# Splitting the tap sums in two and moving four early steps in a fused convolution and maxout kernel

## The chip, the cores and the metric

The kernel runs on one core of one Trainium2 chip. The metric is the time of one execution on the device, in microseconds (us), as the median of several runs; lower is better. A separate execution was profiled: its profile gives the start and the length of nearly every instruction on the core's engines, and of the DMA packets.

The engines are written as in the profile: PE multiplies matrices (PEld is its loading of the stationary operand), DVE works on vectors, ACT applies functions and copies, POOL and SP here mostly issue DMAs.

## The reference

The input x has 8 sequences of 4160 rows with 192 values. Each row also has 8 heads x 7 logits. A softmax over the 7 logits gives weights for the row itself and the six before it, head by head; then the 33280 rows go through a layer that takes the maximum of two products:

```python
w = np.exp(weight_gen - max); w = w / (sum over the 7 taps + 1e-09)
out = np.einsum('bshk,bskhg->bshg', w, x_unf)      # 7 taps, 8 heads x 24 values
...
h1 = x @ w1                                        # 192 -> 1024
h2 = x @ w2
g = np.maximum(h1, h2)
return (g @ w_out).astype(np.float32)              # 1024 -> 192
```

## The kernel before

**Tiling.** Each of the 128 partitions holds 260 consecutive rows ("columns" of 128 rows each). Batches of 16 columns are the unit of the softmax; units of 4 columns (the first 32 columns, units 0 to 7) or 8 columns (the rest) are the unit of the convolution. One column's worth of the layer is a *tile*: 260 tiles, worked off in groups, of two tiles up to tile 15 (groups 0 to 7) and of three tiles after that.

**The layer.** The maximum is written as h1 + relu(h2 - h1). `hid_tile(t)` (line 352) makes the tile's 1024 hidden values on PE from the convolved columns `yt` and from `wd` = w2 - w1, `relu(rd, t, n)` (line 362) takes them through ACT into `rd`, and the result of a column is 16 products of `rd` with `wo`, the bf16 copy of w_out (line 392), plus 3 products of `yt` with `w10` = w1 @ w_out (line 405). Halves of the PE array work side by side on 64 rows each, so `wd` exists with its halves of rows in place (blocks 0 to 2) and swapped (blocks 3 to 5). `halves_swapped(frm, bank)` makes a swapped block: one product into a PSUM bank, then a copy on ACT (lines 677 and 679).

**The convolution.** Per batch: `exp_sum` (ACT, line 162), `red` (DVE, 180), `ln` (ACT, 186), `shift` (DVE, 191), `weights` (ACT, 202: the normalised weights in bf16, twice each), `mul` (DVE, 218: all 7 taps of a unit into `m_t`). From unit 8 on DVE adds up the taps (`adds`, 244 to 253) and a DMA transposes the sum (262). For units 0 to 7 `sum_transpose(u)` (line 285) does both on PE: for each of six blocks k, seven taps and two halves it is a 64-column product of `m_t` with the identity (line 296), 84 products in all (48 for unit 5, whose taps DVE adds up in part), and ACT then copies the result to `yt` (line 304).

**What sets the order.** Every engine works off its instructions in the order in which the program states them; waits come from the data, from PSUM banks that must be read out before they are filled again, and from explicit ties: `behind(first, load)` makes a DMA's issue wait for `first`. The first 16 tiles and their softmax are written out by hand, from line 698 on. PSUM in that stretch is two pools of two buffers each, `h` (hidden tiles; also `pw`) and `o` (`yps` of a tap sum, `op_ps` of results, `other`, `tp`). In `hidden(g, ...)` (line 543) the order on PE is: the group's first hidden tile, the first half of the previous results (`out_first`), the second hidden tile, the second half (`out_second`), the copy of the results by ACT (`evac`, line 478), and then what the caller passes as `between`. A callback `ahead` runs between the second relu and `out_second`.

The places that the change touches, before it:

- POOL issues the DMA of `wo` (line 706) right behind a load of x, with no wait; `wo` is first read by `out_hidden_only(OUTS[3])` at line 781.
- Lines 722 to 744: on ACT the order is relu of tile 0, relu of tile 1, `ln(0)`, `exp_sum(1)`, the copy of swapped block 4 (`halves_swapped(1, other)`), `weights(0, 8)`, the copy of unit 1's sum, `ln(1)`, relu of tile 2. `hid_tile(2)` is the first that reads block 4.
- Lines 778 to 786: `sum_transpose(2)` as a whole, then `out_hidden_only`, `hid_tile(6)`, `out_hidden_rest`, relu of tile 6, `hid_tile(7)`.
- Lines 889 to 896: the tap sums of units 4, 6 and 7 stand in `between` of groups 4, 6 and 7. In group 4, `weights(1, 12)` is the `ahead` step, and `exp_sum(2)` and `red(2)` stand in `between`, behind the copy of the results.

Of the kernel before, what the change touches and what calls it, by code (L numbers as in the profile page):

```python
# [9 lines left out]
FP32 = mybir.dt.float32  # L10
# [13 lines left out]
def kernel(  # L24
# [133 lines left out]
    def exp_sum(b, i=0, of=1):  # L158
        if i == 0:
            e_ts[b] = pe_.tile([P, BATCHES[b][1] * WGC], FP32, name="e_t", tag="e")  # L160
        w = BATCHES[b][1] * WGC // of
        return nc.scalar.activation(out=e_ts[b][:, i * w:(i + 1) * w], in_=wg_ts[b][:, i * w:(i + 1) * w], func=AF.Exp)  # L162
# [15 lines left out]
    def red(b, i=0, of=1):  # L178
        hs, at, ap = part(b, i, of)
        nc.vector.reduce_sum(out=sums(b, hs), in_=_sub(e_ts[b], at, ap), axis=AX.X)  # L180

    def ln(b, i=0, of=1):
        if i == 0:
            s_ts[b] = psm.tile([P, BATCHES[b][1] * H], FP32, name="ln_t", tag="ln")
        hs = part(b, i, of)[0]
        nc.scalar.activation(out=s_ts[b][:, hs], in_=sums(b, hs), func=AF.Ln)  # L186
# [7 lines left out]
    def weights(b, o):  # L194

        w = dict(pieces(b))[o]
        if b not in en_ts:
            en_ts[b] = pen.tile([P, 16 * WGC * 2], BF16, name="en_t", tag="en")
        J = 2 if w == 4 and b < 2 else 1
        N = w * H // J  # L200
        for j in range(J):
            nc.scalar.activation(  # L202
                out=_sub(en_ts[b], (o * WGC + j * N * K) * 2, [[2 * N, K], [2, N], [1, 2]]),
                in_=_sub(wg_ts[b], (o * H + j * N) * K, [[1, K], [K, N], [0, 2]]), func=AF.Exp,
            )
# [78 lines left out]

    def sum_transpose(u, taps=range(K), amid=lambda: None, now=True):

        b, o, n = UNITS[u]
        assert n == 4
        yps = ps["r" if "r" in ps else "o"].tile([P, 1024], FP32, name="yps", tag="op")
        for k in range(6):  # L290
            if k == 3:
                amid()
            for t in taps:
                for r in range(2):
                    at = (K * o + t * n) * D + k * P
                    nc.tensor.matmul(  # L296
                        yps[:, r * 512 + k * 64:r * 512 + (k + 1) * 64],
                        lhsT=m_t[half(r), at:at + P], rhs=ident[half(r), half(r)],
                        start=(k == 0 and t == taps[0]), stop=(t == taps[-1]),
                        skip_group_check=True,  # L300
                    )
        def copy():
            yt = pyt.tile([P, 8 // 2 * 3 * P], BF16, name="yt", tag="yt")
            yt_of[u] = nc.scalar.copy(out=_sub(yt, 0, [[64, 2], [P, 6], [1, 64]]),  # L304
                                      in_=_sub(yps, 0, [[512, 2], [64, 6], [1, 64]]))
            yt_ts[u] = yt

        if now:
            copy()
        return copy  # L310


# [31 lines left out]
    def hid_tile(t):  # L344


        u = TILES[t][0]
        fs, w = chunks(t)
        for f in fs:
            for s in range(3):  # L350
                for j in range(2):
                    nc.tensor.matmul(  # L352
                        hid_out(t, f, j), lhsT=wd_at(j, s, f // 4, f % 4 * P, P),
                        rhs=_sub(yt_ts[u][half(j), :], (s + j) % 3 * P, [[3 * P, w // P], [1, P]]),
                        start=(f == fs[0] and s == 0), stop=(f == fs[-1] and s == 2),
                        skip_group_check=True,
                    )

    def relu(rd, t0, n):

        (hd, at), k = hd_at[t0], rd_at[t0][1]
        relu_of[t0] = nc.scalar.activation(out=rd[:, k * 1024:(k + n) * 1024], in_=hd[:, at:at + n * 1024],  # L362
                                           func=AF.Relu)
# [68 lines left out]
    def out_hidden_rest(now, go):  # L432

        for c in now[::2]:
            for f in range(FCH):
                for j in range(2):
                    mm = out_hidden(c + j, f, j, False, False)
                    if c == now[0] and f == 0:
                        tc.add_manual_dep(mm.ins, go.ins.name, SYNC, reason="bank of the other half")
# [13 lines left out]
    def relay(last, eng=nc.scalar):  # L453

        go = eng.nop()
        for mm in last:
            tc.add_manual_dep(go.ins, mm.ins.name, SYNC, reason="bank of the other half")
        return go
# [81 lines left out]
        for c in now:  # L540
            op_at[c // 2] = tile_, (c - now[0]) // 2 * D

    def hidden(g, now=(), between=lambda: None, beside=lambda: None, ahead=lambda: None):


        t0, n = GROUPS[g]
        rd = room(g)
        for t in range(t0, t0 + n - 1):
            hid_tile(t)
        if now:  # L550
            out_room(now, "ab" if n == 1 and "ab" in ps else None)
            last = out_first(now)
        if len(now) > 2:
            relu(rd, t0, n - 1)
        else:
            for t in range(t0, t0 + n - 1):
                relu(rd, t, 1)
        if now:
            go = relay(last)
        hid_tile(t0 + n - 1)  # L560
        if len(now) > 2:
            beside()
        relu(rd, t0 + n - 1, 1)
        ahead()
        if now:
            out_second(now, go)
            evac(now[0] // 2, len(now) // 2)
        between()
        if len(now) <= 2:
            beside()  # L570
# [30 lines left out]
    with tc.tile_pool(name="pstage", bufs=1) as pstage:  # L601
# [82 lines left out]
        def w1_transposed():  # L684

            tp = ps["o"].tile([P, 1024], FP32, name="tp", tag="op")[:, :].bitcast(BF16)
            for at, kind, nr in ((0, "E", P), (P, "T", 64)):
                for fi in range(FCH):
                    o = fi // 4 * 1024 + fi % 4 * D
                    rows, c = (slice(0, P), fi) if kind == "E" else (half(fi // 4), fi % 4)  # L690
                    nc.tensor.matmul(
                        tp[:, o + at:o + at + nr],
                        lhsT=w1[kind][rows, c * P:(c + 1) * P],
                        rhs=ident[rows, rows], is_transpose=True, skip_group_check=True,
                    )
            return tp
# [5 lines left out]
        for h in range(2):  # L702
            nc.gpsimd.dma_start(out=w1["T"][half(h), :], in_=bass.AP(
                tensor=moe_w1.tensor, offset=P * F + h * HF, ap=[[F, 64], [1, HF]]))
        load_x(0, 12, 4)
        nc.gpsimd.dma_start(
            out=wo[:, :].rearrange("p (f d) -> p f d", d=D),
            in_=bass.AP(tensor=moe_w_out.tensor, offset=0, ap=[[D, P], [P * D, FCH], [1, D]]),
        )
        mul_pair(0, 4, 0, 0, 4)  # L710
        sum_transpose(0, amid=lambda: halves_swapped(0, warm[:, 512:1024]))
        keep_warm(2)
# [10 lines left out]
        relu(rd, 0, 1)  # L723
        behind(relu_of[0], load_x(1, 0, 8))
        hid_tile(1)
        relu(rd, 1, 1)
        ln(0, 1, 2)
        shift(0, 1, 2)
        exp_sum(1)
# [1 line left out]
        other = ps["o"].tile([P, 1024], FP32, name="other", tag="op")  # L731
        halves_swapped(1, other[:, 0:512])
        weights(0, 8)
        red(1)
        mul(0, 8)
        features()
# [1 line left out]
        rd = room(1)  # L738
        hid_tile(2)
        relu(rd, 2, 1)  # L740
        tp = w1_transposed()
        hid_tile(3)
        relu(rd, 3, 1)
# [32 lines left out]
        hid_tile(5)  # L776
        relu(rd, 5, 1)
        behind(relu_of[5], load_wg(2, nc.gpsimd))
        sum_transpose(2)
        out_room(OUTS[3])  # L780
        go = out_hidden_only(OUTS[3])
        rd = room(3)
        hid_tile(6)
        out_hidden_rest(OUTS[3], go)
        relu(rd, 6, 1)
        hid_tile(7)
        pw = w10_product()
        weights(1, 4)
# [35 lines left out]
    def with_maximum():  # L824

        with tc.tile_pool(name="again", bufs=1) as pa, \
# [54 lines left out]
            with tc.For_i(0, CPP, 1) as c:  # L881
# [4 lines left out]
                nc.vector.tensor_copy(out=halo, in_=pr[:, 0:PAD * D])  # L886

    none = lambda: None
    early = {
        3: (none, rest_of_1),  # L890
        4: (lambda: (behind(relu_of[8], load_x(2, 0, 8, halo=False)), exp_sum(2), red(2),
                     sum_transpose(4), behind(yt_of[4], load_wg(4, nc.gpsimd)), ln(2)), end_of_1),
        5: (lambda: (exp_sum(3), red(3), sum_transpose(5, LEFT), weights(2, 0)), none),
        6: (lambda: (weights(2, 8), ln(3), sum_transpose(6)), none),
        7: (lambda: (behind(relu_of[14], load_x(2, 8, 8)), sum_transpose(7)), none),
    }

    NOW = (22, 28, 40, 49, 106, 118)
# [73 lines left out]
    for g in range(4, len(GROUPS)):  # L972
        if GROUPS[g][1] == 3 and "c" not in ps:
            later_ps()
        tiles = [t for t in range(GROUPS[g][0], sum(GROUPS[g])) if t >= 16]
        if g == 9:
            behind(relu_of[16], load_x(3, 0, 8))
        if g in early:
            hidden(g, OUTS[g], early[g][0], ahead=lambda: {4: lambda: weights(1, 12), }.get(g, none)())
            early[g][1]()  # L980
            steps(g, tiles)
        else:
            hidden(g, OUTS[g], beside=lambda: steps(g, tiles))
# [37 lines left out]
```

## Time and profile before

| | |
|---|---|
| three timed runs | 410.93, 410.9, 411.96 us (median 410.93) |
| the profiled execution | 410.43 us, of which 408.7 are the span of instructions |
| PE busy | 397.6 us (97%) |
| DVE busy | 376.4 us (92%) |
| ACT busy | 355.6 us (87%) |
| PE clock granted | 0.999 on the mean |
| tap sums on PE (line 296) | 636 products, 11.1 us busy |
| DMA of `wo` | 1, 384 KB in bf16, 7.7 us from issue to landing |

How to read it: the busy time of PE is modelled, with matmuls overlapping, so it shows where PE had work and not whether it ran at its peak. A wait is found in the timeline, as idle time ahead of an instruction, together with the engine or the DMA that ended it. "issue" there means that nothing in the profile explains the wait. A group of instructions at one line is merged in the timeline into one row: start, length, engine, line, what it writes and reads, how many, and, in brackets, the idle time before it.

### The profile page before, as it was taken

What the parts mean: (1) busy time and instruction counts of PE and PEld (TensorE: products, weight loads), DVE (VectorE), ACT (ScalarE), POOL (GpSimd) and SP (SyncE); (2) the same over time, 40 slices, a digit from 0 to 9 for tenths busy, and PEclk for the clock granted to TensorE, in tenths of its full rate; (3) what the DMA queues carried; (4) which work ended last, traced back from release to release, by engine and by line L of the source; (5) the groups of instructions that cost most, each with busy time, mean ns of one, the idle gap of its engine ahead of it and who ended that gap; (6) DMA issues with size and microseconds to landing.
All of it is one profiled execution on the core that took longest, in us unless ns stands there. A gap on an engine that the chain in (4) does not pass through costs nothing.

```text
span 408.7 us, 16198 instructions
## 1 busy us (share of the span) xinstructions
PE 397.6 (97%) x7415; PEld 317.6 (78%) x7415; DVE 376.4 (92%) x227; ACT 355.6 (87%) x421; POOL 81.4 (20%) x108
## 2 busy tenths in 40 slices
PE   7889999999999999999999999999999999999995
PEld 2688999777777877777787778777777777777795
DVE  6898999999999999999999999999999999999500
ACT  3899998999889998898988999998999889898872
POOL 1412013122221112222210121220122222320000
PEclk9999999999999999999999999999999999999999
DMA  8957297757648764875777578478558656944423
GB/s 253 251 128 199 62 206 164 184 135 175 168 96 212 190 149 104 245 201 70 237 197 109 115 232 202 82 230 191 109 111 244 162 96 205 186 98 140 116 76 123
DMA packets 63510, 65.92 MB, mean 161 GB/s; under 512 B 47825, under 2 KB 52561, under 8 KB 63440
## 3 DMA queue, kind: packets, MB, share of 16 engines
q1 hardware_dynamic: 54464, 40.15, 36.0%
q0 software_dynamic: 8832, 24.63, 29.7%
q8 instruction: 58, 0.95, 0.9%
q10 hardware_dynamic: 144, 0.10, 0.1%
q14 instruction: 12, 0.10, 0.1%
HBM read 37.33 MB, written 25.56 MB: 154 GB/s over the span
## 4 chain that ended last, share of the span: by engine, by line
PE 88%; ACT 8%; issue 2%; DVE 1%; DMA 1%; ACTq 0%; DVEq 0%
PE op_ps L392 39%; PE hd L352 38%; PE op_ps L405 7%; ACT rd_t L362 4%; PE yps L296 1%; PE hdp L352 1%; ACT e_t L162 1%; DVE m_t L227 1%; ACT o_t L478 1%; ACT en_t L202 1%; DMA wg_t<-in_weight_gen_dram 1%; ACT yt L304 1%; DVE s_first L180 0%; PE pw L755 0%; ACT xb_t L150 0%
## 5 line engine op out<-in xcount | busy, mean ns | idle before, releaser
L362 ACT ACTIVATE rd_t<-hd 128x1024 bf16<-128x1024 f32 (+1 forms) x206 | 234.6, 1187 | 26.6 <-PE hd L352 25.3
L392 PE MATMUL op_ps<-wo,rd_t 64*128 64x192 bf16 x4160 | 210.4, 243 | 1.0 <-issue 1.0
L392 PEld LDWEIGHTS <-rd_t 64*128 64x128 bf16 x4160 | 180.9, 94 | 16.5 <-issue 1.1
L352 PE MATMUL hd<-yt,wd 64*128 64x512 bf16 (+1 forms) x1584 | 187.5, 360 | 0.7 <-ACT rd_t L362 0.4
L218 DVE TENSOR_TENSOR m_t<-xb_t,en_t 128x10752 bf16<-128x10752 bf16 (+1 forms) x35 | 181.6, 5192 | 1.0 <-ACT en_t L202 1.0
L352 PEld LDWEIGHTS <-wd 64*128 64x128 bf16 x1776 | 94.2, 94 | 44.2 <-issue 3.8
L270 POOL CAST gate<-yt 128x1 f32<-128x1 bf16 x29 | 42.5, 1465 | 257.0 <-DMA yt<-y_t 257.0
L244 DVE TENSOR_TENSOR m_t<-m_t 128x4608 bf16<-128x4608 bf16 (+1 forms) x30 | 74.1, 2471 | 0.1
L478 ACT COPY o_t<-op_ps 128x384 f32<-128x384 f32 (+1 forms) x99 | 57.3, 589 | 12.5 <-PE op_ps L392 12.5
L405 PE MATMUL op_ps<-w,yt 64*128 64x192 bf16 x768 | 54.6, 243 | 0.1
L405 PEld LDWEIGHTS <-yt 64*128 64x128 bf16 x768 | 37.8, 94 | 16.4 <-issue 1.3
L250 DVE TENSOR_TENSOR m_t<-m_t 128x3072 bf16<-128x3072 bf16 (+1 forms) x29 | 50.0, 1723 | 0.1
L202 ACT ACTIVATE en_t<-wg_t 128x896 bf16<-128x896 f32 (+2 forms) x45 | 35.9, 822 | 0.7 <-DVE wg_t L191 0.7
L253 DVE TENSOR_TENSOR y_t<-m_t 128x1536 bf16<-128x1536 bf16 (+1 forms) x29 | 27.3, 941 | 0.5
L133 POOL DMA_DIRECT2D xb_t<-in_x_dram x34 | 18.3, 538 | 29.4 <-ACT rd_t L362 20.6
L191 DVE TENSOR_TENSOR wg_t<-wg_t,ln_t 128x280 f32<-128x280 f32 (+5 forms) x46 | 22.1, 481 | 1.2 <-ACT ln_t L186 1.2
L162 ACT ACTIVATE e_t<-wg_t 128x896 f32<-128x896 f32 (+2 forms) x18 | 16.3, 904 | 1.3 <-DMA wg_t<-in_weight_gen_dram 1.3
L362 ACT ACTIVATE rd_t<-hdp 128x1024 bf16<-128x1024 f32 x16 | 15.9, 1046 | 0.9 <-PE hdp L352 0.9
L180 DVE TENSOR_REDUCE s_rest<-e_t 128x64 f32<-128x448 f32 (+2 forms) x27 | 16.3, 604 | 0.0
L352 PE MATMUL hdp<-yt,wd 64*128 64x256 bf16 x192 | 13.4, 269 | 1.8 <-ACT e_t L162 1.2
L296 PE MATMUL yps<-ident,m_t 64*128 64x64 bf16 x636 | 11.1, 190 | 1.1 <-issue 1.0
L296 PEld LDWEIGHTS <-m_t 64*128 64x128 bf16 x636 | 10.4, 95 | 2.1 <-issue 1.5
(56 smaller groups left out, 80.9 us busy)
## 6 DMA issues: line engine op xcount, KB each, us to landing
out_dram<-o_t SPq DMA_DIRECT2D x22, 768.0 KB, 5.3
xb_t<-in_x_dram POOLq DMA_DIRECT2D x30, 384.0 KB, 5.2
out_dram<-o_t SPq DMA_DIRECT2D x20, 384.0 KB, 3.1
wg_t<-in_weight_gen_dram POOLq DMA_DIRECT2D x13, 448.0 KB, 5.3
xb_t<-xb_t POOLq DMA_DIRECT2D x15, 288.0 KB, 5.3
xb_t<-in_x_dram POOLq DMA_DIRECT2D x4, 192.0 KB, 5.5
xs<-in_x_dram SPq DMA_DIRECT2D x1, 576.0 KB, 3.9
ws0E<-in_moe_w_dram SPq DMA_DIRECT2D x2, 256.0 KB, 5.4
```

The lines of the kernel that those rows point to most:

```text
L202: nc.scalar.activation(out=_sub(en_ts[b], (o * WGC + j * N * K) * 2, [[2 * N, K], [2, N], [1, 2]]), in_=_sub(wg_ts[b], (o * H + j * N) * K ...
L218: return nc.vector.tensor_tensor(out=m_out, in0=x_in, in1=_sub(en_ts[b], o * WGC * 2, [[2, K * n * H], [0, G // 2], [1, 2]]), op=ALU.mult,)
L244: nc.vector.tensor_tensor(out=taps(0, 1, 3), in0=taps(0, 1, 3), in1=taps(3, 1, 3), op=ALU.add)
L250: nc.vector.tensor_tensor(out=taps(0, 2, 2), in0=taps(0, 2, 2), in1=taps(1, 5, 2), op=ALU.add)
L253: nc.vector.tensor_tensor(out=_sub(y_ts[b], o * D, [[64, 2], [P, 3 * w // 2], [1, 64]]), in0=taps(0, 1, 1), in1=taps(2, 1, 1), op=ALU.add,)
L270: nc.gpsimd.tensor_copy(out=gate, in_=yt[:, 0:1])
L296: nc.tensor.matmul(yps[:, r * 512 + k * 64:r * 512 + (k + 1) * 64], lhsT=m_t[half(r), at:at + P], rhs=ident[half(r), half(r)], start=(k == ...
L352: nc.tensor.matmul(hid_out(t, f, j), lhsT=wd_at(j, s, f // 4, f % 4 * P, P), rhs=_sub(yt_ts[u][half(j), :], (s + j) % 3 * P, [[3 * P, w // ...
L362: relu_of[t0] = nc.scalar.activation(out=rd[:, k * 1024:(k + n) * 1024], in_=hd[:, at:at + n * 1024], func=AF.Relu)
L392: return nc.tensor.matmul(op_out(c), lhsT=rd[half(r), k * 1024 + at:k * 1024 + at + P], rhs=wo[half(r), f * D:(f + 1) * D], start=start, s ...
L405: nc.tensor.matmul(op_out(c + j), lhsT=yt_ts[u][half(j), (3 * i + (s + j) % 3) * P:(3 * i + (s + j) % 3 + 1) * P], rhs=w10[half(j), s * D: ...
L478: nc.scalar.copy(out=_sub(o, c % 24 * D, [[D, len(qs)], [h * D, 2], [1, D]]), in_=_sub(tile_, at + (qs[0] - p) * D, [[D, len(qs)], [512, 2 ...
```

## The change

1. `sum_transpose` is cut into `sum_part(u, k0, k1)`, which makes the products of blocks k0 to k1, and the copy, which can be stated later.
2. Unit 2: blocks 0 to 2 stay where the sum was; blocks 3 to 5 go between `hid_tile(6)` and `out_hidden_rest`; the copy to `yt` goes behind the relu of tile 6.
3. Units 4, 6 and 7: blocks 0 to 2 go ahead of the group's second hidden tile (a new callback `amid`), blocks 3 to 5 and the copy stay behind the results. Unit 5 is left whole.
4. The relu of tile 1 goes behind the copy of swapped block 4 and behind `weights(0, 8)`.
5. In group 4 `exp_sum(2)` and `red(2)` go ahead of the results, and `weights(1, 12)` goes behind the sum's copy.
6. The DMA of `wo` is issued behind the relu of tile 2 and not at the start.

```diff
+    def sum_part(u, k0, k1, taps=range(K)):
 ...
+        if k0 == 0:
+            yps_of[u] = ps["r" if "r" in ps else "o"].tile([P, 1024], FP32, name="yps", tag="op")
+        yps = yps_of[u]
+        for k in range(k0, k1):
             for t in taps:
 ...
-    def hidden(g, now=(), between=lambda: None, beside=lambda: None, ahead=lambda: None):
+    def hidden(g, now=(), between=lambda: None, beside=lambda: None, ahead=lambda: None, amid=lambda: None):
 ...
         if now:
             go = relay(last)
+        amid()
         hid_tile(t0 + n - 1)
 ...
         load_x(0, 12, 4)
-        nc.gpsimd.dma_start(
-            out=wo[:, :].rearrange("p (f d) -> p f d", d=D),
-            in_=bass.AP(tensor=moe_w_out.tensor, offset=0, ap=[[D, P], [P * D, FCH], [1, D]]),
-        )
         mul_pair(0, 4, 0, 0, 4)
 ...
         hid_tile(1)
-        relu(rd, 1, 1)
         ln(0, 1, 2)
 ...
         weights(0, 8)
+        relu(rd, 1, 1)
         red(1)
 ...
         relu(rd, 2, 1)
+        behind(relu_of[2], nc.gpsimd.dma_start(
+            out=wo[:, :].rearrange("p (f d) -> p f d", d=D),
+            in_=bass.AP(tensor=moe_w_out.tensor, offset=0, ap=[[D, P], [P * D, FCH], [1, D]]),
+        ))
 ...
-        sum_transpose(2)
+        features = sum_part(2, 0, 3)
         out_room(OUTS[3])
         go = out_hidden_only(OUTS[3])
         rd = room(3)
         hid_tile(6)
+        sum_part(2, 3, 6)
         out_hidden_rest(OUTS[3], go)
         relu(rd, 6, 1)
+        features()
         hid_tile(7)
 ...
-        4: (lambda: (behind(relu_of[8], load_x(2, 0, 8, halo=False)), exp_sum(2), red(2),
-                     sum_transpose(4), behind(yt_of[4], load_wg(4, nc.gpsimd)), ln(2)), end_of_1),
+        4: (lambda: (behind(relu_of[8], load_x(2, 0, 8, halo=False)),
+                     rest_of_sum(4), weights(1, 12), behind(yt_of[4], load_wg(4, nc.gpsimd)), ln(2)), end_of_1),
         5: (lambda: (exp_sum(3), red(3), sum_transpose(5, LEFT), weights(2, 0)), none),
-        6: (lambda: (weights(2, 8), ln(3), sum_transpose(6)), none),
-        7: (lambda: (behind(relu_of[14], load_x(2, 8, 8)), sum_transpose(7)), none),
+        6: (lambda: (weights(2, 8), ln(3), rest_of_sum(6)), none),
+        7: (lambda: (behind(relu_of[14], load_x(2, 8, 8)), rest_of_sum(7)), none),
 ...
-            hidden(g, OUTS[g], early[g][0], ahead=lambda: {4: lambda: weights(1, 12), }.get(g, none)())
+            hidden(g, OUTS[g], early[g][0], ahead=lambda: (exp_sum(2), red(2)) if g == 4 else None,
+                   amid=lambda: first_of_sum(g) if g != 5 else None)
```

More of the change, by code (lines that the diff above doesn't have):

```diff
@@ L285, in sum_transpose @@
     def sum_transpose(u, taps=range(K), amid=lambda: None, now=True):
+        copy = sum_part(u, 0, 3, taps)
+        amid()
+        sum_part(u, 3, 6, taps)
+        if now:
+            copy()
+        return copy
+    yps_of = {}
+    def sum_part(u, k0, k1, taps=range(K)):
         b, o, n = UNITS[u]
         assert n == 4
[L289 to L292, printed above, removed]
+        if k0 == 0:
+            yps_of[u] = ps["r" if "r" in ps else "o"].tile([P, 1024], FP32, name="yps", tag="op")
+        yps = yps_of[u]
+        for k in range(k0, k1):
             for t in taps:
@@ L306, in copy @@
             yt_ts[u] = yt
-        if now:
-            copy()
         return copy
@@ L559, in hidden @@
             go = relay(last)
+        amid()
         hid_tile(t0 + n - 1)
@@ L888, with first_of_sum, rest_of_sum @@
     none = lambda: None
+    begun = {}
+    def first_of_sum(u):
+        begun[u] = sum_part(u, 0, 3)
+    def rest_of_sum(u):
+        sum_part(u, 3, 6)
+        begun[u]()
     early = {
         3: (none, rest_of_1),
-        4: (lambda: (behind(relu_of[8], load_x(2, 0, 8, halo=False)), exp_sum(2), red(2),
-                     sum_transpose(4), behind(yt_of[4], load_wg(4, nc.gpsimd)), ln(2)), end_of_1),
+        4: (lambda: (behind(relu_of[8], load_x(2, 0, 8, halo=False)),
+                     rest_of_sum(4), weights(1, 12), behind(yt_of[4], load_wg(4, nc.gpsimd)), ln(2)), end_of_1),
         5: (lambda: (exp_sum(3), red(3), sum_transpose(5, LEFT), weights(2, 0)), none),
-        6: (lambda: (weights(2, 8), ln(3), sum_transpose(6)), none),
-        7: (lambda: (behind(relu_of[14], load_x(2, 8, 8)), sum_transpose(7)), none),
+        6: (lambda: (weights(2, 8), ln(3), rest_of_sum(6)), none),
+        7: (lambda: (behind(relu_of[14], load_x(2, 8, 8)), rest_of_sum(7)), none),
     }
```

## The prediction

> **What bounds the kernel now.** I read the page's busy shares first, then the table of stretches, the timeline of the first 62 us, and last the trace's own records of DMA packets and semaphores.
>
> ```profile
> PE 397.6 (97%) x7415; PEld 317.6 (78%) x7415; DVE 376.4 (92%) x227; ACT 355.6 (87%) x421; POOL 81.4 (20%) x108
> q8 instruction: 58, 0.95, 0.9%
> ```
>
> ```profile
> 15.00:17.50 2.50, 1.32 (x68) 1.06 (x60) 1.44 (x3) 2.50 (x6) 0.55 (x1) 1.00 1.22 197
> 22.50:25.00 2.50, 1.49 (x58) 1.37 (x51) 2.50 (x2) 2.50 (x5) 0.53 (x1) 1.00 0.05 18
> 35.00:40.00 5.00, 4.01 (x141) 3.79 (x135) 4.32 (x3) 4.54 (x9) 0.54 (x1) 1.00 0.88 205
> 90.00:120.00 30.00, 30.00 (x514) 23.02 (x512) 29.96 (x17) 28.10 (x34) 7.96 (x8) 1.00 0.59 146
> ```
>
> The columns are stretch, length, busy PE, PEld, DVE, ACT, POOL, clock, DMA share, GB/s. From 90 on, PE and DVE are both full, so whatever PE is late at the end of the start-up stays to the end. DVE gives nothing back: by the semaphore records the transposed sums of tile 224 landed at 344.32 and PE first read them at 344.42. All parts of the change lie before 48.7 us. There PE is idle three times for over a microsecond, in the first three stretches:
>
> ```profile
> 16.11 0.95 ACT L162 ACTIVATE e_t<-wg_t 128x896 f32<-128x896 f32 x1
> 16.95 0.58 ACT L679 CAST wd<-other 128x512 bf16<-128x512 f32 x1
> 17.48 0.83 PE L352 MATMUL hdp<-yt,wd 64*128 64x256 bf16 x12 [1.18 <-ACT e_t L162]
> ...
> 18.90 1.96 ACT L362 ACTIVATE rd_t<-hdp 128x1024 bf16<-128x1024 f32 x2
> ...
> 21.30 1.53 ACT L748 COPY w1t<-tp 128x768 bf16<-128x768 bf16 x2
> ...
> 23.68 0.47 PE L296 MATMUL yps<-ident,m_t 64*128 64x64 bf16 x20 [1.01 <-issue]
> ...
> 23.97 1.50 PE L392 MATMUL op_ps<-wo,rd_t 64*128 64x192 bf16 x32
> 24.05 0.53 POOL L133 DMA_DIRECT2D xb_t<-in_x_dram  x1 [4.14 <-ACT rd_t L362]
> ```
>
> ```profile
> 37.34 0.84 PE L392 MATMUL op_ps<-wo,rd_t 64*128 64x192 bf16 x16 [0.99 <-issue]
> ```
>
> **What the idle times are.** PE has 14830 instructions and queue q8 brings 58 packets of 16 KB, so 256 instructions a packet. Counting PE's instructions, the waits that end at 17.48, 23.68, 37.34 and 55.27 fall on numbers 449, 705, 1473 and 2497, which are 449 plus 0, 1, 4 and 8 times 256. Their packets ended at 16.00, 22.20, 35.81 and 53.86: each wait ended 1.41 to 1.53 us behind its packet. So these are waits for PE's own instructions, the one at 17.48 too, although the profile names `exp_sum`. A packet that comes in time is no wait. The packets queue behind data: that for 705 started at 21.24, behind `wo` (landed 20.75).
>
> **The change part by part.** The times below are on the clock of the profiled execution.
>
> *Relu of tile 1 behind the copy of block 4.* PE gains almost nothing. Its instructions up to 449 keep their order and their packet (15.03 to 16.00, ahead of `wo`, issued at 13.00), so `hid_tile(2)` starts at 17.48 again; only its third weight load, which waited for the copy (17.54), can come 0.05 earlier. ACT loses. Steps between its starts, from the rows: relu 0.92, ln 0.145, exp 0.84, copy 0.465, weights 0.6. With relu 1 gone from the front, exp ends at 16.16, but `other` is finished by PE only at 16.30, so the copy starts at 16.36, and ACT has a hole of 0.3. From there all follows without a gap: relu 1 at 17.4, the copy of unit 1 at 18.3, relu 2 at 19.22 to 20.26 (before 18.90 to 19.94). `hid_tile(4)` and `(5)` wait for the banks of relus 2 and 3, as they did, so PE is 0.3 late at 21.86. DVE runs `mul(0, 8)` 0.55 earlier; nobody waits for that.
>
> *`wo` behind relu 2.* POOL issued 0.28 us behind the end of its relu at 15.45, 24.05 and 25.57, so `wo` goes out at 20.55 and holds POOL for 0.95, as before. No other POOL step is late: the next load waits for relu 4 (24.1). When does `wo` land? No row has it alone. The nearest is the x load at 24.05, as many bytes (768 KB read, 384 KB written) on an idle queue: first packet 1.23 us behind the issue, landed at 28.45, 4.4 behind. From below: 1.23 and the 2.0 us by which `wo` landed behind the load ahead of it (20.75 against 18.74), 3.2 in all. From above: the x load at 34.20 under other traffic, 5.9. I take 4.3, near the first, so 24.85; the ends are 23.75 and 26.45. `out_hidden_only`, its first reader, started at 23.97; now it starts at 24.9, **0.9 later**. Behind it wait PE's whole queue and, through banks, ACT.
>
> [...]
>
> *Unit 2's sum in halves.* The first 42 products take 0.63 (15 ns each), 21.86 to 22.49. Number 705 now lies within `out_hidden_only`; without `wo` ahead of it its packet comes some 2 us earlier (19.2 to 20.2, usable 21.65), so the wait of 1.2 goes. Late next would be the bank of `tp`, read out by the `w1t` copies at 22.83 and now at 23.15; with `wo` at 24.85 that is covered. The other 42 products now stand behind `out_hidden_only`: **0.63 later** for `out_hidden_rest`, which moves from 25.95 to 24.9 + 1.32 + 0.66 + 0.63 = 27.5. From 23.97 to 36.11 PE had no wait that could take this up. ACT follows PE: the copy of unit 2 goes to about 28.0 and `weights(1, 4)` to 28.7, so `mul(1, 4)` starts at 29.4 and not 27.8; its reader, the sum of unit 5 at 39.31, has room.
>
> *Units 4, 6, 7 in halves.* The same products between the same ends: zero for PE as long as no wait hangs on it. In group 4 the second hidden tile, and relu 9 on ACT, come 0.4 later (34.2 for 33.8, before the shift).
>
> *`exp_sum(2)` and `red(2)` ahead.* DVE's wait of 0.68 at 36.67 mostly goes, and ACT's 0.47 ahead of `ln(2)`. But `weights(1, 12)` now comes last, at about 37.9 for 35.4, so `mul(1, 12)` starts 0.25 later. The results' copy moves from 35.28 to about 36.0, and its bank is needed at 35.95: 0.6 late, hidden under the instruction wait that ends at 37.34. That wait costs 0.6 less if the packet comes early, and otherwise stays: its trigger and the logits' load ahead of it both hang on PE's stage and shift together. All else up to 48.7, `weights(2, 0)` for DVE's long chain included, hangs on PE's stage too.
>
> Sum: 0.9 + 0.63 = 1.5 on 410.43, **411.9** for the profiled execution. That execution stands 0.5 under the median of the timed runs, so 412.4 there. `wo` at its ends gives 0.45 and 3.1, which is 411.4 and 414.0.
>
> **The rivals.**
>
> *(a) `wo` lands by about 24.2, little is lost.* The DMA queue has drained by then, which speaks for it; the x load with 4.4 speaks against. With `wo` at 23.9 the loss is 0.6; had it come by 23.15, PE would start on the bank and gain 0.1. 410.8 to 411.8, say 411.5.
>
> *(b) Faster: PE's instruction packets come in time.* It is one mechanism: a queue free of `wo`'s 1024 rows, and short bursts of PE instructions in place of 84 products at 15 ns, could let all of the packets arrive. Then the waits at 37.34 (0.6 of it) and 55.27 (0.47) go with that at 23.68. It decides only if `wo` lands by 23.15, 2.6 us from its issue: 0.1 + 0.6 + 0.47 = 1.2 gained, 409.7. For it speaks that four waits sit on such numbers; against it, that no load landed in under 3.2.
>
> *(c) The PE clock falls.* PE would be idle from 22.49 to 24.9. The rows grant full clock through waits of 1.6, and half from 408.13, 3.6 us behind the last product (404.5). At the start full clock came 3.7 us behind the first product (5.36 against 1.64). A fall would cost half of such a stretch, 1.9: 414.3. An idle time of 2.4 lies between 1.6 and 3.6.
> [...] No run here shows the threshold itself.
>
> **How the numbers follow.** Forecast, `wo` late by 0.3 to 1.5: 0.57. (a) 0.24. (b) 0.11. (c), or `wo` later than that: 0.08. A measurement of this kernel tells a difference of about 0.3%, 1.23 us, from none. The forecast lies above that with 0.46 of its 0.57, and (c) wholly: slower 0.54. (a) and the rest of the forecast: same 0.35. (b): faster 0.11. The range, 410.2 to 414.0, takes in `wo`'s ends and (a), and leaves out most of (b) and (c).
>
> **What would show it.** Right: `wo` issued near 20.55 and landed near 24.85; `out_hidden_only` waiting for that DMA; no wait at number 705; the hole of 0.3 on ACT ahead of the copy of block 4; `hid_tile(2)` still at 17.48; `mul(1, 4)` near 29.4; everything from 48.7 on shifted by one amount. Wrong: `out_hidden_only` starting before 23.7, `hid_tile(2)` well before 17.48, or the wait at number 1473 gone. I would also be wrong if the collisions of transposes with stores near 344 and 356, where DVE's lead is 0.1, fall otherwise after the shift.

## The result, and the profile after

The changed kernel takes **415.18 us** (median of 6 runs, 413.35 to 417.09) beside 410.94 for the kernel before (6 runs, 410.45 to 411.96): a ratio of 1.010, 95% interval 1.007 to 1.0129. It is slower, as forecast, but by 4.2 us, not by 1.5, and outside of the range.

The profiled execution of the changed kernel took 413.35 us (span 411.6) against 410.43, so +2.92. The lines of the code have moved: the numbers that the prediction uses are 10 to 11 higher now (tap sums 307, their copy 316, hidden tiles 362, relu 372, products with `wo` 402, results' copy 488, swapped copies 690, the DMA of `wo` 748).

The starts of the same PE steps in the two profiled executions show where it came from:

| step on PE | before | after | late by |
|---|---|---|---|
| first hidden tile | 12.84 | 13.07 | 0.23 |
| `hid_tile(2)` | 17.48 | 16.93 | -0.55 |
| `hid_tile(4)` | 19.99 | 20.54 | 0.55 |
| `out_hidden_only` | 23.97 | 25.98 | 2.01 |
| `out_hidden_rest` | 25.95 | 28.57 | 2.62 |
| `hid_tile(12)` | 40.01 | 42.56 | 2.55 |
| `hid_tile(14)` | 44.12 | 46.94 | 2.82 |
| `hid_tile(16)` | 48.66 | 52.04 | 3.38 |
| tile 24 | 59.27 | 62.27 | 3.00 |
| last product | 404.27 | 407.20 | 2.93 |

The two steps of the forecast are here, the first twice as large: +1.78 beyond the late start at `out_hidden_only`, +0.61 for the second half of unit 2's sum. From tile 12 to tile 16 another 0.83 is lost, of which 0.4 comes back at tile 24, where an instruction wait of before (0.47, at 54.8) is gone. After that nothing changes, so DVE gave nothing back, as forecast.

The timeline of the kernel after around the first two steps (start, length, engine, line, what, and the idle time ahead with what ended it):

```profile
16.58 0.59 ACT L690 CAST wd<-other 128x512 bf16<-128x512 f32 x1 [0.19 <-PE other L688]
16.93 1.00 PE L362 MATMUL hdp<-yt,wd 64*128 64x256 bf16 x12 [0.39 <-issue]
20.54 1.75 PE L362 MATMUL hdp<-yt,wd 64*128 64x256 bf16 x24 [0.98 <-ACT rd_t L372]
20.78 0.90 POOL L748 DMA_DIRECT2D wo<-in_moe_w_out_dram  x1 [0.76 <-ACT rd_t L372]
25.98 1.49 PE L402 MATMUL op_ps<-wo,rd_t 64*128 64x192 bf16 x32 [3.08 <-DMA wo<-in_moe_w_out_dram]
30.51 2.96 DVE L218 TENSOR_TENSOR m_t<-xb_t,en_t 128x5376 bf16<-128x5376 bf16 x1 [2.63 <-ACT en_t L202]
```

`wo` was issued where the forecast had it (20.78 for 20.55, the start being 0.23 later) and PE waited for it. The chain of waits of the same kernel gives the time from issue to landing:

```profile
20.50 0.28 issue
20.78 5.15 DMA wo<-in_moe_w_out_dram
25.98 1.49 PE op_ps L402 x32
```

5.15 us, where the forecast had 4.3. The packets show where the time goes: `wo` comes as 1024 rows. The first of its packets began 1.6 us behind the issue, 0.7 behind the end of the 0.90 that POOL spends on issuing it, and from there to the end of the last it took 3.25. The lower bound's 2.0 was only by how much `wo` landed behind its neighbour in a queue that was already running.

The page's cost list carries the same mark: the products with `wo` had 1.0 us of idle time ahead of them before, put down to "issue", and now

```profile
L402 PE MATMUL op_ps<-wo,rd_t 64*128 64x192 bf16 x4160 | 210.3, 243 | 3.4 <-DMA wo<-in_moe_w_out_dram 3.1
```

The loss between tiles 12 and 16 is mostly a wait that was not there before. The same copy and the sum of unit 7 in the kernel before, with no idle time ahead of the sum:

```profile
45.92 0.85 ACT L304 CAST yt<-yps 128x768 bf16<-128x768 f32 x1
...
47.22 1.41 PE L296 MATMUL yps<-ident,m_t 64*128 64x64 bf16 x84
```

In the kernel after:

```profile
47.15 0.47 ACT L488 COPY o_t<-op_ps 128x384 f32<-128x384 f32 x1
...
48.63 0.80 ACT L316 CAST yt<-yps 128x768 bf16<-128x768 f32 x1
```

```profile
47.91 0.84 PE L402 MATMUL op_ps<-wo,rd_t 64*128 64x192 bf16 x16
49.48 0.79 PE L307 MATMUL yps<-ident,m_t 64*128 64x64 bf16 x42 [0.73 <-ACT yt L316]
```

The first half of unit 7's sum needs a PSUM buffer of the pool `o`. That pool has two: one is filled with the group's results, the other still holds unit 6's sum until ACT has copied it (48.63 to 49.43). Before, the whole sum of unit 7 stood behind the results, some 1.3 us further on in PE's order, and the copy was done by then. Unit 6's first half begins at 44.41, just behind the copy of unit 5's sum (43.55 to 44.35), which fits the 0.27 of the 0.83 that is lost between tiles 12 and 14.

**The timed median lies 1.83 above the profiled execution.** That part no timeline of this execution shows; the mean clock of each of the six runs shows most of it:

| run | 413.35 (the profiled) | 414.63 | 414.96 | 415.4 | 415.49 | 417.09 |
|---|---|---|---|---|---|---|
| mean granted clock | 0.998 | 0.994 | 0.994 | 0.995 | 0.995 | 0.996 |

One stretch of 3.4 us at half speed is 0.004 of the span and costs 1.7 us, by an estimate from the stretch at half clock that e4 shows below (3.42 us, measured cost 1.67). Five of the six runs are at or under 0.996; of the 87 runs of the kernel before that were taken beside the experiments, two are. So the accounting of 4.24 is: 2.92 of the profile, less 0.51 by which the profiled execution before lay under its own median, plus 1.83 between the profiled run and the median, for which one fall of the clock (1.7) is the likely reason. It does not explain every run: that of 417.09 lies 3.7 above the profiled one with the loss of one fall, so some 2 us of it stay open.

### The profile page after: what moved, and what is told of

The parts are those of the page before. It is cut to its first block, busy times and chain, and to the rows that moved or that the text cites. A ratio compares the mean times of both kernels' runs of the same rounds, so it can differ in the third digit from the quotient of the medians.

```text
span 411.6 us, 16200 instructions
## 1 busy us (share of the span) xinstructions
PE 398.9 (97%) x7415; PEld 317.6 (77%) x7415; DVE 376.8 (92%) x227; ACT 355.9 (86%) x421; POOL 78.4 (19%) x108
## 4 chain that ended last, share of the span: by engine, by line
PE 88%; ACT 6%; DMA 2%; issue 2%; DVE 1%; SPq 0%; ACTq 0%; DVEq 0%
PE op_ps L402 39%; PE hd L362 38%; PE op_ps L415 7%; ACT rd_t L372 3%; PE yps L307 2%; DMA wo<-in_moe_w_out_dram 1%; DMA xs<-in_x_dram 1%; PE hdp L362 1%; DVE m_t L227 1%; ACT yt L316 1%; ACT en_t L202 1%; ACT o_t L488 0%; PE pw L766 0%; ACT xb_t L150 0%; ACT wd L690 0%
## 5 line engine op out<-in xcount | busy, mean ns | idle before, releaser
L270 POOL CAST gate<-yt 128x1 f32<-128x1 bf16 x29 | 39.2, 1351 | 260.1 <-DMA yt<-y_t 260.1
```

Source lines behind the costliest of these rows:

```text
L270: nc.gpsimd.tensor_copy(out=gate, in_=yt[:, 0:1])
```

## The experiments

Each expectation names its own theories; A is everywhere the reading that the profiles gave up to then. Ratios are to the kernel before, run on the same chip in the same batch: 410.45 us for e1 to e4 (17 runs), 411.01 for e5, e6, b1 and b2 (35 runs), 410.41 for the other four (35 runs). A ratio is not the quotient of the two medians and can differ from it by 0.001. No kernel leaves work out; e3 adds products that are overwritten.

### The wait for `wo` and the clock

**e1: the changed kernel with the DMA of `wo` at its old place.**

```diff
         load_x(0, 12, 4)
+        nc.gpsimd.dma_start(out=wo..., in_=moe_w_out...)
...
-        behind(relu_of[2], nc.gpsimd.dma_start(out=wo..., in_=moe_w_out...))
```

> The changed kernel with the DMA of wo back at its old place, behind the load of x. Theory A (the loss is the wait for wo, some of it through the PE clock that falls in the wait): out_hidden_only starts at about 23.4 on the read-out of tp and not at 25.98, no PE wait over 1 us near 23, mean clock 0.998 in all runs; what stays is the second half of unit 2's sum (0.6 later) and the bank wait ahead of unit 7's first half (0.75), less the instruction wait near 55 (0.47): 411.3, between 410.6 and 411.9. Theory B (the new order of sums and ACT steps costs most, and the wait for wo only takes the place of other waits): 413 or more.

411.15 us (410.61 to 412.17, 12 runs), ratio 1.0012 [0.9994, 1.0031], mean clocks 0.997 to 1.0. Without the tie some 0.5 us of loss are left of 4.2 by the ratio, whose interval holds 1, and the clock stays up. `out_hidden_only` starts at 23.26, behind the `w1t` copies as the prediction had it for an early `wo`, but the wait of units 6 and 7 stays:

```profile
23.26 1.50 PE L402 MATMUL op_ps<-wo,rd_t 64*128 64x192 bf16 x32 [0.53 <-ACT w1t L759]
...
46.78 0.79 PE L307 MATMUL yps<-ident,m_t 64*128 64x64 bf16 x42 [0.61 <-ACT yt L316]
```

**e2: the kernel before with only the DMA of `wo` behind relu 2.**

```diff
-        nc.gpsimd.dma_start(out=wo..., in_=moe_w_out...)
...
         relu(rd, 2, 1)
+        behind(relu_of[2], nc.gpsimd.dma_start(out=wo..., in_=moe_w_out...))
```

> The kernel before with only the DMA of wo tied to the relu of tile 2. Theory A: issued at 20.2, landed 5.15 later (as measured in the changed kernel) at 25.4, so out_hidden_only starts 1.45 later than 23.97: 412.4, with the instruction wait at number 705 gone; PE is idle for some 2.5 us, so a fall of the clock by one window (mean 0.994 to 0.996 for 0.998, some 1.7 us more) comes in fewer runs than in the changed kernel, or in none. Theory B: 411, within 0.3%.

413.54 (412.26 to 414.64, 6 runs), ratio 1.0077 [1.0051, 1.0102]. Issue at 20.40, landing at 25.58, 5.18 behind it:

```profile
20.40 0.90 POOL L737 DMA_DIRECT2D wo<-in_moe_w_out_dram  x1 [0.36 <-ACT rd_t L362]
...
25.63 1.49 PE L392 MATMUL op_ps<-wo,rd_t 64*128 64x192 bf16 x32 [2.49 <-DMA wo<-in_moe_w_out_dram]
```

The six runs part by their clocks: 412.26, 412.83 and 413.11 at 0.998 to 1.0, near theory A's 412.4; 413.97, 414.55 and 414.64 at 0.994 to 0.996. So one edit out of six carries most of the loss, and its clock part comes and goes from run to run.

**e3: the changed kernel, with nine products of 512 columns in the wait for `wo`.** They go into the PSUM buffer that the results then overwrite.

```diff
+        idle = op_at[OUTS[3][0] // 2][0]
+        for _ in range(9):
+            nc.tensor.matmul(idle[:, 0:512], lhsT=ident[:, 0:P], rhs=..., start=True, stop=True)
         go = out_hidden_only(OUTS[3])
```

> The changed kernel with nine extra products of 512 columns on PE (identity by identity, into the bank that out_hidden_only writes next, overwritten by it) ahead of out_hidden_only, so that PE works through most of the wait for wo. They add work and take none away. Theory A: the clock stays full after the start in all runs (mean 0.998), and the median falls from 415.2 to about 413.4, the time of the one run of the changed kernel whose mean clock was 0.998. Rival C (the runs above 413.4 had wo, or other transfers, land later): the median stays at 415 and the mean clock at 0.994 to 0.996.

414.16 (413.64 to 414.57, 6 runs), ratio 1.0085 [1.0063, 1.0108]; all mean clocks 0.998 to 1.0. The products fill 2.10 us of the wait, `out_hidden_only` starts where it did in the kernel after (26.02 for 25.98), and the spread of 3.7 us shrinks to 0.9. With added work the median is 1.0 lower; against the kernel before of the same batch it is 3.7 slower where the kernel after was 4.2, and the two intervals overlap. So it is the clocks that tell the two apart: none of six runs fell, against five of six. It came out 0.8 above the expected 413.4, and one line says where:

```profile
23.40 2.10 PE L794 MATMUL op_ps<-ident 128*128 128x512 bf16 x9 [0.54 <-ACT w1t L759]
26.02 1.50 PE L402 MATMUL op_ps<-wo,rd_t 64*128 64x192 bf16 x32 [0.52 <-DMA wo<-in_moe_w_out_dram]
...
40.15 0.38 PE L362 MATMUL hdp<-yt,wd 64*128 64x256 bf16 x3 [1.49 <-issue]
```

Nine products and their weight loads are 18 instructions, so number 1473, at which an instruction packet ends, falls 18 earlier in the work, inside `hid_tile(10)`; its packet also ended 0.45 later (38.83 for 38.38). From tile 10 to 12 it takes 5.25 us here and 4.66 in the kernel after: 0.59.

In the kernel before PE had no idle time at six of the first ten of these ends, and 0.2 to 1.2 us at the other four; the longest such wait in these runs is 1.8 (in e5).

**e4: the changed kernel with unit 7's sum left whole.**

```diff
-        7: (lambda: (..., rest_of_sum(7)), none),
+        7: (lambda: (..., sum_transpose(7)), none),
...
-                   amid=lambda: first_of_sum(g) if g != 5 else None)
+                   amid=lambda: first_of_sum(g) if g in (4, 6) else None)
```

> The changed kernel with unit 7's sum whole again, behind the results of group 7. Theory A: the wait of 0.73 ahead of the first half (for the copy of unit 6's sum) goes, and PE reaches the first tile of group 8 some 0.8 earlier; the instruction wait near 55 (0.47) may come back: 0.3 to 0.8 under the changed kernel, 414.4 to 414.9. If the wait were only moved to the next bank: no difference.

414.66 (413.85 to 414.75, 6 runs), ratio 1.0093 [1.0071, 1.0116], inside what was expected. But four of the six runs are at 0.994 to 0.996, as in the kernel after most were, and one took 414.59 at a mean clock of 1.0, which the clock does not explain; so the times alone do not price unit 7. The profile does: tiles 14 to 16 take 4.69 us (5.10 in the kernel after, 4.54 before). Its profiled execution, 414.67, caught the fall of the clock. The stretches on either side of it (start and end, length, busy PE, PEld, DVE, ACT, POOL, then the clock, DMA share, GB/s):

```profile
22.58:25.99 3.41, 0.22 (x9) 0.15 (x6) 3.41 (x2) 2.98 (x5) 0.68 (x2) 1.00 1.12 123
25.99:29.41 3.42, 3.42 (x44) 2.95 (x42) 1.64 (x1) 0.00 (x0) 0.41 (x1) 0.50 0.96 220
29.41:32.82 3.41, 3.41 (x98) 3.14 (x95) 0.78 (x1) 2.85 (x5) 0.00 (x0) 1.00 0.05 21
```

The first is the wait for `wo`, at full clock; in the second PE works without a pause at half clock; then it is full again. The same 32 products show it:

```profile
25.84 2.64 PE L402 MATMUL op_ps<-wo,rd_t 64*128 64x192 bf16 x32 [3.19 <-DMA wo<-in_moe_w_out_dram]
...
30.10 1.49 PE L402 MATMUL op_ps<-wo,rd_t 64*128 64x192 bf16 x32
```

From `out_hidden_only` to `hid_tile(8)` it takes 9.49 us here and 7.82 in the kernel after, at full clock: the fall costs 1.67. Why not there, with a wait of 3.08? The stretches at full clock in these profiles are multiples of 3.413 us (20.480, 399.359, 402.773, 406.186: 6, 117, 118 and 119 of them), so here the clock changed on a grid of 3.413 us, at a phase that differs between executions (the full clock begins at 5.36 in the profile before and at 7.45 in that after). In the kernel after the bounds fell so that both stretches over the wait held work:

```profile
21.11:24.52 3.41, 1.70 (x60) 1.38 (x54) 3.15 (x2) 3.41 (x8) 0.57 (x1) 1.00 0.74 96
24.52:27.93 3.41, 1.95 (x44) 1.90 (x46) 3.36 (x2) 1.28 (x3) 1.09 (x2) 1.00 1.02 145
```

With 1.70 and 1.95 us busy nothing fell; with 0.22 of 3.41 it did. The ends of the profiles, where PE runs out of work, narrow this down, since there too the stretch at full clock ends with a whole window. The last window but one in e1 and the last before the fall in b4:

```profile
403.34:406.75 3.41, 1.46 (x36) 1.23 (x30) 0.00 (x0) 1.08 (x3) 0.00 (x0) 1.00 0.66 222
402.33:405.74 3.41, 1.43 (x36) 1.20 (x30) 0.00 (x0) 1.04 (x3) 0.00 (x0) 1.00 0.67 225
```

The first was followed by full clock, the second by half. In all fourteen profiles every window of a full-clock stretch with 1.46 us or more of PE work was followed by full clock, and every one with 1.43 or less by half (PE's busy time being the modelled one).

### The other edits, alone

**e5: the kernel before with only the relu of tile 1 moved.**

```diff
         hid_tile(1)
-        relu(rd, 1, 1)
...
         weights(0, 8)
+        relu(rd, 1, 1)
```

> The kernel before with only the relu of tile 1 moved behind the copy of block 4 and weights(0, 8). Theory A: relus 2 and 3 come 0.3 later, so hid_tile(4) starts 0.3 later, but PE runs into the instruction wait at number 705, whose end (about 23.7) does not hang on PE, and nothing is left of it at out_hidden_only: no difference, 410.5 (409.9 to 411.1). Theory B (the step itself costs PE or ACT time that stays): 411 or more, with out_hidden_only 0.3 later.

411.57 (409.77 to 412.27, 12 runs), ratio 1.0000 [0.9981, 1.0018]. `hid_tile(4)` starts 0.7 later, and the instruction wait behind it takes that up:

```profile
20.71 1.75 PE L352 MATMUL hdp<-yt,wd 64*128 64x256 bf16 x24 [0.95 <-ACT rd_t L362]
...
23.68 0.47 PE L296 MATMUL yps<-ident,m_t 64*128 64x64 bf16 x20 [0.29 <-issue]
23.97 1.25 PE L392 MATMUL op_ps<-wo,rd_t 64*128 64x192 bf16 x26
```

23.68 and 23.97 are the times of the kernel before to the digit. Further on this profile, of an execution of 412.08, loses 0.8 at number 1473, whose packet began 0.97 later (35.73 for 34.76), and more behind it; no run shows whether that belongs to the edit. The ratio is the expected no difference; the median lies above the 409.9 to 411.1 that were expected, in a batch whose kernel before took 411.01.

**e6: e1 with the relu of tile 1 back too** (what is left are the halves, and group 4's exponential).

```diff
+        relu(rd, 1, 1)
         ln(0, 1, 2)
...
         weights(0, 8)
-        relu(rd, 1, 1)
```

> The changed kernel with wo at its old place and the relu of tile 1 back, so that only the halves and the third exponential are left of the change. Theory A: the copies of tp end 0.3 earlier than in the run with wo alone put back, and out_hidden_only, which waits for them, starts at 22.9 and not at 23.3: 0.3 to 0.4 under that run, 410.8. Theory B (out_hidden_only would then wait for the instructions at number 705 or for something else): the same time as that run, 411.15.

411.11 (410.4 to 412.34, 12 runs), ratio 0.9999 [0.9983, 1.0015]. Inconclusive: the 0.3 to 0.4 us that it was to have over e1 is not to be told from nothing. In its profile `out_hidden_only` starts at 23.63, which is 0.1 earlier than in e1 once the later start (13.38 for 12.90 at the first hidden tile) is taken off.

**b1: the kernel before with only unit 2's sum in halves.**

```diff
-        sum_transpose(2)
+        features = sum_part(2, 0, 3)
...
         hid_tile(6)
+        sum_part(2, 3, 6)
         out_hidden_rest(OUTS[3], go)
         relu(rd, 6, 1)
+        features()
```

> The kernel before with only unit 2's sum in halves. Theory A: the wait at number 705 goes, because the number now falls 0.9 us into out_hidden_only; out_hidden_only starts on the read-out of tp at 22.9, out_hidden_rest at 25.5 for 25.95, and the gain of 0.45 stays to the end: 410.0 (409.6 to 410.4). Theory B (the wait is not for instructions and only moves): 410.5.

410.66 (410.21 to 413.01, 12 runs), ratio 0.9992 [0.9975, 1.0009]. In its profile the wait at number 705 is gone and `out_hidden_only` starts at 23.37, but the second half takes 0.6 of that back: `hid_tile(8)` starts at 31.20 (31.19 before), in an execution that began 0.43 later, so 0.4 gained. The timed interval holds both this gain and none.

**e7: the kernel before with only `exp_sum(2)` and `red(2)` ahead of group 4's results, and `weights(1, 12)` behind the sum's copy.**

```diff
-        4: (lambda: (..., exp_sum(2), red(2), sum_transpose(4), ...), end_of_1),
+        4: (lambda: (..., sum_transpose(4), weights(1, 12), ...), end_of_1),
...
-  ahead=lambda: {4: lambda: weights(1, 12), }...
+  ahead=lambda: {4: lambda: (exp_sum(2), red(2)), }...
```

> The kernel before with only exp_sum(2), red(2) and weights(1, 12) moved. Theory A: the results' copy of group 4 comes later, but PE reaches number 1473 before its packet in any case: no difference (ratio 0.999 to 1.001), with PE's wait near 36 split between the bank and the packet. Theory B (the bank wait adds to the packet's): 0.6 slower, ratio 1.0015.

411.0 (409.59 to 412.48, 12 runs), ratio 1.0014 [1.0001, 1.0027]. Theory A, no difference, missed by a little; B had the size but not the way. The interval only just leaves out 1. The wait near 37 stays (0.82 for 0.99), and a second appears, at number 1729:

```profile
37.06 0.84 PE L392 MATMUL op_ps<-wo,rd_t 64*128 64x192 bf16 x16 [0.82 <-issue]
...
41.88 0.72 PE L352 MATMUL hdp<-yt,wd 64*128 64x256 bf16 x10 [0.30 <-issue]
```

The load of logits that is tied to unit 4's copy is issued earlier (36.75 for 37.62), and the packet of these instructions begins later (39.42 for 38.46). But e5, which leaves the exponential where it was, has the same wait of 0.30 at 1729, while of the runs that move it e6 has one of 0.66 and e1, d1 and b4 have none. So this profile does not show that the edit makes the wait.

**d1: e1 with units 6 and 7 whole.**

```diff
-        6: (lambda: (weights(2, 8), ln(3), rest_of_sum(6)), none),
-        7: (lambda: (..., rest_of_sum(7)), none),
+        6: (lambda: (weights(2, 8), ln(3), sum_transpose(6)), none),
+        7: (lambda: (..., sum_transpose(7)), none),
...
-                   amid=lambda: first_of_sum(g) if g != 5 else None)
+                   amid=lambda: first_of_sum(g) if g == 4 else None)
```

> The changed kernel with wo at its old place and the sums of units 6 and 7 whole. Theory A (the halves of units 6 and 7 make PE wait for the copy of the sum before): from the first tile of group 6 to that of group 8 PE takes 8.6 us, as in the kernel before (8.65), and not 9.3 as in the run with wo alone put back; the time 0.3 to 0.6 under that run's 411.15, so 410.7, ratio 0.999 to 1.001. Theory B (the waits there come from ACT's lateness, not from the halves): 9.3 again.

410.55 (409.88 to 411.61, 12 runs), ratio 1.0009 [0.9997, 1.0021]. Tiles 12 to 16 take 8.82 us (e1 9.34, before 8.65): in the profiles the halves of these two units cost 0.5 of the 0.7 there. The timed ratios, 1.0009 and e1's 1.0012, do not tell the two apart. A smaller wait, of the results' copy, comes up in their place:

```profile
44.90 0.42 PE L415 MATMUL op_ps<-w,yt 64*128 64x192 bf16 x6 [0.22 <-ACT o_t L488]
```

### Versions that might beat both

**b2: the kernel before, with a load of logits tied to relu 6 and not to the `w10` copies**, so that it and the packet behind it go out earlier.

```diff
-        behind(w10_of[-1], load_wg(3, nc.gpsimd))
+        behind(relu_of[6], load_wg(3, nc.gpsimd))
```

> The kernel before with one tie changed: the load of batch 3's logits waits for the relu of tile 6 (27.2) and not for the copies of w10 (30.7). Theory A (the wait of 1.23 at number 1473 is for an instruction packet that queues behind this load): the load has landed by 31.5, the packet triggered near 31.3 starts 1 to 2 us earlier than 34.76, the wait goes or falls under 0.3, and the time by 0.9 to 1.2: 409.4. Theory B (the wait is for something else on PE or ACT): the wait stays and the time with it, 410.5.

410.22 (409.51 to 411.01, 12 runs), ratio 0.9977 [0.9961, 0.9993]. The instruction wait ahead of 36.79 is 0.43 and not 0.99, and tile 12 starts at 39.47 (40.01 before); then a wait for the results' copy gives it back, and tile 16 starts at 48.67 (48.66 before):

```profile
36.79 0.84 PE L392 MATMUL op_ps<-wo,rd_t 64*128 64x192 bf16 x16 [0.43 <-issue]
...
45.01 0.42 PE L405 MATMUL op_ps<-w,yt 64*128 64x192 bf16 x6 [0.38 <-ACT o_t L478]
```

**b3: b2's line together with b1's edit.**

> The kernel before with unit 2's sum in halves and the load of batch 3's logits behind the relu of tile 6. Theory A (each takes away a wait for an instruction packet, at numbers 705 and 1473; what PE gains at 1473 is partly spent on the results' copy of group 6, which ACT makes no earlier): 0.4 from the first and 0.5 of PE's 1.2 from the second, so 409.9 where the kernel before has 410.9, ratio 0.997 to 0.999. Theory B (ACT sets the pace of groups 4 to 7, so that no gain ahead of it reaches the end): ratio 1.0.

410.41 (409.79 to 411.24, 12 runs), ratio 0.9997 [0.9983, 1.0010]: no gain that can be told from none, so theory A's 0.997 to 0.999 is not borne out.

**b4: b3 with e7's edit as well.**

> The kernel of the run above with exp_sum(2) and red(2) ahead of the results of group 4 as well. Theory A: the wait of 0.47 on ACT ahead of ln(2) goes, so the relus of group 5 come 0.4 earlier now that PE no longer waits for instructions there: 0.2 to 0.4 under the run above, ratio 0.996 to 0.998. Theory B: the results' copy of group 4 comes 0.6 later and PE waits for its bank, which takes the gain: the same as the run above or 0.2 more.

410.0 (409.63 to 411.8, 12 runs), ratio 0.9993 [0.9981, 1.0004]. Tile 16 starts at 48.30 in its profile, 0.36 earlier than before, but the interval holds 1, and it is not to be told from b3. So of the three, b2 alone was faster outside its interval, its own profile shows no gain at tile 16, and b3, which holds the same line, does not repeat it. Whether b2 gains anything stays open.

## Why the prediction was wrong

**Right: the place and the sign.** `out_hidden_only` waited for `wo`, issued as forecast; e2 and e1 show that this edit is most of the loss (1.0077 alone; 1.0012 without it). The one run of the kernel after that kept its clock, 413.35, lies inside the range of 410.2 to 414.0; less the 1.7 of a fall, four of the other five would too.

**Failed: "I take 4.3, near the first".** The landing took 5.15 (5.18 to 5.26 in e2, e3 and e4). I took the x load at 24.05 as the nearest row since it has as many bytes. But from 24.9 to 28.6, the time of that load, the queue moved 186 packets, all except 16 of them of 2 to 8 KB; `wo` has 1024 of 384 bytes, and took 3.25 us from its first packet to its last, where the 128 packets of that load took 2.81. The first packet, too, came 1.61 and not 1.23 behind the issue, and not for a queue that was still full: in e3 it came 1.63 behind, though the packets ahead had ended 0.37 before it. POOL spends 0.90 on issuing `wo` and 0.53 on issuing x, and in both the first packet came 0.7 behind the end of that. So the step that failed is the row taken for `wo`; that the short rows are what makes the packets take longer is argued from these two loads, and no run varied the rows alone. The upper end of 5.9 held this; the term was +0.9 and measured +1.78.

**Right: +0.63 for the second half of unit 2's sum.** 0.61, and no wait up to 36 took it up.

**Failed: rival (c) at a price of 1.9 and, with a still later `wo`, a chance of 0.08.** The price was nearly right (1.67 in e4). The chance was an estimate of mine, when no run showed at what wait the clock falls, and it failed for two reasons. The idle time was taken from the 4.3 and so was 2.4 where it was 3.08. And I asked between which two lengths of idle time the threshold lies, when in these profiles what counted was how little work a window of 3.413 us held (1.43 us or less ahead of half clock, 1.46 or more ahead of full). (The 1.6 was misread too: it is the idle time ahead of the first product, before the clock records begin; the longest wait at full clock in the profile before is 1.18.) With the bound near 1.45 us of work, a wait must take up some 1.96 of one window. By an estimate from these two figures, with full work on both sides of the wait, a wait of 2.4 does so at 0.55 of the phases, one of 2.49 at 0.58 and one of 3.08 at 0.75. By the mean clocks it was 3 of 6 runs in e2 (2.49), and 5 of 6 in the kernel after (3.08) and 4 of 6 in e4 (3.19). So even on the forecast's own landing time the fall was about as likely as not. e3, which fills the wait with useless work and loses the fall, shows this cause apart from the wait itself, though the run of 417.09 and e4's 414.59 at full clock hold something more that no run explains.

**Failed: "zero for PE as long as no wait hangs on it", for units 4, 6 and 7.** The condition was stated and not followed up for units 6 and 7. Stated earlier, the first half needs its PSUM buffer earlier, and ACT's copy of the sum before it had not read it out: 0.73 at 49.48. Tiles 12 to 16 took 0.83 longer; d1's profile gives 0.5 of e1's 0.7 to these two halves.

**The relu of tile 1: right in the sum, wrong on the way.** The hole on ACT was 0.19 for 0.3, and e5 gives 1.0000. But "`hid_tile(2)` still at 17.48" failed: its instruction packet ran from 14.55 to 15.53, not 15.03 to 16.00, and the tile started 0.55 earlier. It changed nothing, since PE then waited for relu 2 (0.98 at 20.54).

**Instruction packets: right as a mechanism.** The wait at number 705 went, though its packet came 1.0 earlier (20.21 to 21.17) and not 2. In the kernel after the waits at these numbers ended 1.40 and 1.52 us behind their packets, over all runs 1.2 to 1.5, and the one at 1473 stayed, split: 0.40 for the results' copy and 0.35 for the packet. `mul(1, 4)` came at 30.51 for 29.4: later by about what `wo` was late.

**The exponential: costed at nothing, measured at 1.0014 alone [1.0001, 1.0027].** Whether that is more than nothing is close, and the cause stays open: in e7's profile a load tied to unit 4's copy goes out earlier and a packet later, but e5's profile has the same wait with the exponential left where it was.

The sum as it should have been, on the profiled execution: 1.78 + 0.61 + 0.83, less 0.38 at tile 24 and 0.07 in between, and 0.23 for the later start, is 3.00 at tile 24 (2.92 for the whole execution); and 1.7 more for the clock in five of the six runs.

## What to carry to other kernels

When a load is tied to a later event, take its landing time from a row with as many packets of the same length, not as many bytes, and count the time that its issue takes: here two loads of 384 KB took 5.15 us (1024 packets of 384 bytes, POOL busy for 0.90 with the issue) and 4.4 us (128 of 3072, 0.53). A new wait of PE of 2.49 to 3.19 us came with a fall of the clock, 1.67 us where it was measured, in 12 of 18 runs (e2, the kernel after and e4, by their mean clocks): ask how much work is left in a window of 3.413 us around it, and look at the mean clock of every timed run and not at the one profile. When an accumulation is stated earlier, its PSUM buffer is needed earlier (PE waited 0.73 us for it here, at unit 7): look up which copy frees it.

## What the runs showed of the hardware

- In e4 a clock window of 3.413 us with 0.22 us of PE work in it was followed by a window at half clock, with full work in it, at a price of 1.67 us. Over all profiles the bound lies between 1.43 us (half clock next, b4) and 1.46 us (full clock next, e1).
- 384 KB of `wo` written as 1024 rows of 384 bytes took 5.15 to 5.26 us from issue to landing (the kernel after, e2, e3, e4); the same bytes of x, as 128 rows of 3072, took 4.4 (the load at 24.05 in the kernel before). Of the difference 0.38 is that the first packet came later, with an issue that holds POOL for 0.90 us and not 0.53.
- With 18 more instructions ahead of it, and a packet of 256 instructions that ended 0.45 later, the wait at number 1473 was 1.49 us in e3 where it had been 0.35 in the kernel after. The packets were fetched at most 281 instructions ahead of their use in the profiles before and after.
